# Fused attention and two MLPs on one core: a scheduling priority for 30 attention steps

## The chip, the cores and the metric

The kernel runs on one core of a Trainium2 chip. The metric is the device time of one execution in microseconds (us). Five engines work side by side, each through its own queue in order: PE (TensorE, matmuls), ACT (ScalarE), DVE (VectorE), POOL (GpSimd) and SP (SyncE, which here only issues DMAs).

## The reference: what is computed

Attention over 4 batches, 8 heads, 576 tokens and head size 64, then two MLPs over the 2304 tokens of width 512:

```python
cum    = np.cumsum(np.log(np.clip(f, 0.0001, 1.0)), axis=-1)
scores = np.where(causal, -1e9, q @ k.T / np.sqrt(D) + cum[..., :, None] - cum[..., None, :])
x = softmax(scores) @ v                        # heads side by side: 2304 x 512
h = x @ w_in                                   # 512 -> 2048
x = (h * np.tanh(np.log1p(np.exp(h)))) @ w_out # 2048 -> 512
h = x @ w2_in                                  # 512 -> 1024
s = h * softmax(h)
out = ((s - s.mean()) / np.sqrt(s.var() + 1e-6) * g_ln) @ w2_out   # 1024 -> 512
```

## The kernel before

Every operand of a matmul is split into two fp16 halves, a high one and a low one, and each product is three matmuls (high by high, high by low, low by high). Work that makes such halves is what ACT, DVE and POOL do most.

**Attention.** A batch is cut into five row tiles of up to 128 tokens. A step handles 4, 2, 1, 1 and 1 heads in row tiles 0 to 4, so a batch has 30 steps, listed in `seq` (L640). A step passes through these parts:

- `step_s` computes scores on PE into one of three PSUM banks `sp0` to `sp2` (L436, L437, L439).
- `step_r` takes the row maximum on DVE (`nm`, L478, and L491/L492 in row tile 4) and the exponentials on ACT (`p`, L480, and L494/L495 in row tile 4).
- `step_h` makes the high half of the probabilities on ACT (`ph`, L518) and the low half on POOL (L519), and issues a transposing DMA from SP (`pT`, L524), for two heads at once in row tiles 2 to 4.
- `step_pv` multiplies by the values on PE (`pv`, L550 to L552), three steps after the scores. After the last head `fin` divides (L565), splits the tile (L568 on DVE, L569 on POOL) and issues the transpose `xT` from SP (L577), which the first MLP reads.

`ahead`, called behind the scores, prepares what comes later: the raw loads of the next tile or batch from SP (`rawq`, `rawk`, `rawv`, L317), the sums of squares of the next batch's keys and values on ACT (`jkk`, `jkv`, L331, called the stats below), and the splits of q, k and v.

**First MLP.** It goes through the tokens in blocks of 256, of 8 pairs of 128 hidden columns each. `up` (tiles `h`, L787) is 24 matmuls for one 128-column half, `mish` turns `h` into `gt` (ACT L799, L800, L805 to L807, L813; DVE L804, L808; POOL L814), and `down` (L831, into `x`) multiplies by the second weight. For block 0 the sums of a weight group are taken up by DVE (L842), and at the end `evac` scales and splits the block's result (DVE L853 to L857 and L860, ACT L859) and stores it from SP (`x2d`, L861). The second MLP runs behind it and fills the time after attention is done.

**Weights of the first MLP.** While batch 0's row tiles 2 and 3 and block 0 of the MLP run, the weights are loaded and converted on DVE (L134, L136, L138), measured on PE (`gram`, L157), bounded on DVE (L172 to L177) and split: the high half on ACT (L199), the low half by two fp32 matmuls L206 and one L207 on PE into a score bank, from which ACT takes it (L208).

**What sets the order.** The program text emits steps of attention, weight work and MLP in turns: before the main loop `n0 + LAG` = 9 steps, then step by step between the halves of `up` and `down`. A scheduler then sorts each engine's instructions once, when the kernel is built: of those that are ready in its own timeline it takes the one with the lowest place in the program. Buffers that are allocated once, such as the three score banks, keep the program's order of use. At run time each engine goes through its queue in that fixed order and waits wherever an operand isn't there.

## Time and profile before

| what | us |
|---|---|
| median of 3 runs | 870.66 |
| lowest and highest run | 867.29, 870.78 |
| the profiled execution | 868.76 |
| its span, first to last instruction | 867.0 |
| PE busy in the span | 766.6 (88%) |
| DVE, ACT, POOL busy | 594.2, 563.7, 394.2 |

Read the span as a sequence of stages: loading and the first two row tiles of batch 0 until about 80 us; row tiles 2 to 4 of batch 0 with the weights and block 0 of the first MLP until about 186 us, when block 1 begins; attention and first MLP side by side until about 545 us; and both MLPs without attention from there to the end.

### The profile page before, as it was taken

Reading aid. Unit: us, or ns where it says so; the run is one execution under the profiler, and the core shown is the slowest. Engines: PE = TensorE matmul, PEld = TensorE weight load, DVE = VectorE, ACT = ScalarE, POOL = GpSimd, SP = SyncE. Lnnn points to the kernel's source line nnn. Section 1 sums busy time; section 2 is a strip of 40 time slices with the busy share of each in tenths; the row PEclk is TensorE's granted clock in tenths of the full one; section 3 lists DMA queues with packets and bytes.
Section 4 is the critical chain, followed back from the end, with each engine's and each line's share of the span. In section 5 each row is a group of like instructions: output and inputs, shape, how many; then the busy total and the mean of one; then the engine's idle time right before and its main releaser. Section 6 shows DMA issues by size and latency. Waiting matters only on the chain.

```text
span 867.0 us, 16642 instructions
## 1 busy us (share of the span) xinstructions
PE 766.6 (88%) x6255; PEld 481.0 (55%) x6255; DVE 594.2 (69%) x1160; ACT 563.7 (65%) x1234; POOL 394.2 (45%) x321
## 2 busy tenths in 40 slices
PE   0468998779999997998889899987999999999998
PEld 0335565557667665676556667654555554444443
DVE  6797954668867898669887654689656454666451
ACT  5648687868878877787876666776965544333331
POOL 2232333447876565765678653226733132012110
PEclk9979999969999999999999999998999999999999
DMA  9998544487799968998797542751022424344443
GB/s 242 228 268 251 175 122 80 87 163 144 151 197 172 163 131 149 169 181 148 164 165 121 113 80 56 191 210 61 26 37 61 97 50 73 86 109 99 107 87 85
DMA packets 328573, 114.90 MB, mean 133 GB/s; under 512 B 317676, under 2 KB 317676, under 8 KB 328492
## 3 DMA queue, kind: packets, MB, share of 16 engines
q1 hardware_dynamic: 328492, 113.84, 63.7%
q8 instruction: 49, 0.80, 0.4%
q14 instruction: 32, 0.26, 0.1%
HBM read 46.59 MB, written 9.55 MB: 65 GB/s over the span
## 4 chain that ended last, share of the span: by engine, by line
PE 40%; DVE 19%; DMA 16%; ACT 9%; issue 9%; POOL 6%; SPq 1%; DVEq 0%; POOLq 0%; ACTq 0%
PE h L1030 10%; PE o L1070 10%; PE x L831 7%; PE h L787 7%; DMA pT<-ph 5%; POOL ph L519 3%; DMA wo_r<-in_moe_w_out_dram 2%; DVE ta L804 2%; POOL gt L814 2%; ACT p L480 2%; DMA xT<-xh 1%; DMA w2i_r<-in_moe_w_in_dram 1%; DVE th L808 1%; DVE vt L215 1%; DVE ph L516 1%
## 5 line engine op out<-in xcount | busy, mean ns | idle before, releaser
L831 PE MATMUL x<-wout,gt 128*128 128x512 f16 x864 | 218.4, 386 | 17.0 <-DVE x2h L860 8.4
L787 PE MATMUL h<-xT,win 128*128 128x256 f16 x1728 | 221.0, 279 | 1.8 <-DMA xT<-xh 1.8
L519 POOL TENSOR_TENSOR ph<-p,ph 128x512 f16<-128x512 f32 (+4 forms) x120 | 155.4, 1301 | 92.0 <-ACT ph L518 42.3
L787 PEld LDWEIGHTS <-win 128*128 128x128 f16 x1728 | 170.0, 100 | 45.1 <-issue 5.5
L814 POOL TENSOR_TENSOR gt<-th,gt 128x512 f16<-128x512 f32 x72 | 92.5, 1286 | 128.7 <-ACT gt L813 122.0
L831 PEld LDWEIGHTS <-gt 128*128 128x128 f16 x864 | 80.5, 99 | 96.4 <-issue 12.5
L1058 POOL TENSOR_TENSOR z<-sl,z 128x1024 f16<-128x1024 f32 x18 | 38.7, 2150 | 138.2 <-DVE s2c L1037 111.3
L1030 PE MATMUL h<-w,x2T 128*128 128x512 f16 x432 | 98.0, 379 | 0.9 <-POOL w L222 0.9
L1070 PE MATMUL o<-wo,zT 128*128 128x512 f16 x432 | 96.5, 379 | 0.5 <-DMA zT<-z 0.5
L550 PE MATMUL pv<-vt,pT 128*128 128x64 f16 (+3 forms) x480 | 68.6, 200 | 23.3 <-DMA pT<-ph 22.9
L808 DVE SCALAR_TENSOR_TENSOR th<-ta,th 128x512 f32<-128x512 f32 x72 | 64.6, 898 | 30.5 <-ACT ta L807 28.0
L436 PE MATMUL sp<-kt,qa 128*128 128x128 f16 (+3 forms) x480 | 68.7, 219 | 15.6 <-ACT p L480 9.6
L480 ACT ACTIVATE p<-sp,nm 64x64 f32<-64x64 f32 (+7 forms) x128 | 61.2, 484 | 27.3 <-DVE nm L478 12.9
L813 ACT CAST gt<-th 128x512 f16<-128x512 f32 x72 | 44.4, 616 | 44.2 <-DVE th L808 42.7
L437 PE MATMUL sp<-kt,qb 67*128 67x128 f16 (+3 forms) x480 | 70.5, 219 | 2.5 <-DMA kt<-dd 2.5
L1030 PEld LDWEIGHTS <-x2T 128*128 128x128 f16 x432 | 42.3, 98 | 51.4 <-issue 1.2
L1070 PEld LDWEIGHTS <-zT 128*128 128x128 f16 x432 | 42.2, 98 | 51.5 <-DMA zT<-z 0.9
L804 DVE TENSOR_SCALAR ta<-ta 128x512 f32<-128x512 f32 x72 | 53.7, 746 | 23.5 <-ACT ta L799 23.2
L550 PEld LDWEIGHTS <-pT 128*128 128x128 f16 (+3 forms) x480 | 44.3, 100 | 45.8 <-DMA pT<-ph 29.6
L552 PE MATMUL pv<-vt,pT 128*128 128x64 f16 (+3 forms) x480 | 67.8, 195 | 0.0
L551 PE MATMUL pv<-vt,pT 128*128 128x64 f16 (+3 forms) x480 | 67.8, 195 | 0.0
L805 ACT ACTIVATE ta<-ta 128x512 f32<-128x512 f32 x72 | 45.3, 631 | 34.0 <-DVE ta L804 33.8
(231 smaller groups left out, 1462.6 us busy)
## 6 DMA issues: line engine op xcount, KB each, us to landing
wi_r<-in_moe_w_in_dram SPq DMA_DIRECT2D x8, 1024.0 KB
wo_r<-in_moe_w_out_dram SPq DMA_DIRECT2D x8, 1024.0 KB
rawk<-in_k_dram SPq DMA_DIRECT2D x25, 256.0 KB
rawv<-in_v_dram SPq DMA_DIRECT2D x25, 256.0 KB
x2d<-x2h SPq DMA_DIRECT2D x18, 256.0 KB
out_dram<-ro SPq DMA_DIRECT2D x18, 256.0 KB
w2i_r<-in_moe_w_in_dram SPq DMA_DIRECT2D x4, 1024.0 KB
w2o_r<-in_moe_w_out_dram SPq DMA_DIRECT2D x4, 1024.0 KB
```

What stands on the lines that cost most here:

```text
L436: nc.tensor.matmul(o, qa[:, h, r0:r1_], kc[:, h, a0:a1], start=True, stop=False)
L437: nc.tensor.matmul(o, qb_[:67, h, r0:r1_], kc[:67, H + h, a0:a1], start=False, stop=(c != i))
L480: nc.scalar.activation(pv[:m, g * (i + 1) * P + off:g * (i + 1) * P + end], s3[:, g, off:end], AF.Exp, bias=nm[:m, g:g + 1], accum_out=rs[ ...
L519: nc.gpsimd.tensor_tensor(p4[:, :, 1], pv3, p4[:, :, 0], op=ALU.subtract)
L550: nc.tensor.matmul(o, pT[a0:a1, k, :m], vh, start=(c == 0), stop=False)
L787: nc.tensor.matmul(ph, win[:, (fi // 4) * NC1 + c, col:col + P], x[:, lx * NC1 + c, :], start=(m == 0), stop=(m == 3 * NC1 - 1))
L804: nc.vector.tensor_scalar(ta, ta, E20, 1.0, op0=ALU.min, op1=ALU.add)
L808: nc.vector.scalar_tensor_tensor(th, ta, 2.5, th, op0=ALU.subtract, op1=ALU.mult)
L814: nc.gpsimd.tensor_tensor(gt[:, 1], th, gt[:, 0], op=ALU.subtract)
L831: nc.tensor.matmul(o, gt[:, lg, n % 2, t * P:(t + 1) * P], wout[:, fi, lw * 512:(lw + 1) * 512], start=(first and m == 0), stop=(last and ...
L1030: nc.tensor.matmul(h[:, half * 512:(half + 1) * 512], x[:, lx * NC1 + c, :], self.w2[:, half * NC1 + c, lw * 512:(lw + 1) * 512], start=(n ...
L1070: nc.tensor.matmul(o, zT[:, lz * NF2 + c, :], self.wo[:, c, lw * 512:(lw + 1) * 512], start=(n == 0), stop=(n == 3 * NF2 - 1))
```

## The change

`tc.high_priority(offset=800)` tells the scheduler to rank what is emitted inside it 800 places earlier than where it stands in the program. The change puts it around all parts of steps 6 to 35: row tiles 2 to 4 of batch 0 (24 steps) and row tiles 0 and 1 of batch 1 (6 steps). Around the scores it also covers `ahead` and the `pv` and `fin` of the step three back. No instruction is added or removed; each engine has the same instructions in another order. Line numbers behind the edits are 2 higher at first and 9 higher from the main loop on (L331 becomes L333, L480 L482, L518 L520, L799 L808).

```diff
+HP = 800
+HPN = 30
...
+    def ahead_of(n):
+
+        return tc.high_priority(offset=HP) if n0 <= n < n0 + HPN else nullcontext()
+
     def slot_pre():
 
         n = pos["k"] - 1
         if 0 <= n < len(seq):
-            step_r(*seq[n])
+            with ahead_of(n):
+                step_r(*seq[n])
 
     def slot_mid():
         n = pos["k"] - 1
         if 0 <= n < len(seq):
-            step_h(*seq[n])
+            with ahead_of(n):
+                step_h(*seq[n])
...
     def slot_pe():
         n = pos["k"]
-        if n < len(seq):
-            step_s(*seq[n])
-            b, i, hs = seq[n]
-            for h in hs:
-                ahead(b, i, h)
-        pvs(n - LAG)
+        with ahead_of(n):
+            if n < len(seq):
+                step_s(*seq[n])
+                b, i, hs = seq[n]
+                for h in hs:
+                    ahead(b, i, h)
+            pvs(n - LAG)
         pos["k"] += 1
```

DVE where the last step of batch 0's row tile 2 takes its maxima (`nm_2_6`, `nm_2_7`: heads 6 and 7; `wo_r_969`, `wo_r_982`: the last two pieces of the down weight), before:

```order
L134 TENSOR_SCALAR wout<-wo_r_969 128x1024
L842 SCALAR_TENSOR_TENSOR acc_1478<-x_0_1_4_1596,rho,acc_1478 128x512
L808 SCALAR_TENSOR_TENSOR th_1694<-ta_1693,th_1694 128x512
L478 TENSOR_REDUCE nm_2_6_1006<-sp_146 128x1
L136 SCALAR_TENSOR_TENSOR wout<-wo_r_969,wout 128x1024
L478 TENSOR_REDUCE nm_2_7_1072<-sp_148 128x1
L134 TENSOR_SCALAR wout<-wo_r_982 128x1024
L425 COPY qb_126<-qa_4_1358 64x8x64
L138 SCALAR_TENSOR_TENSOR wout<-wo_r_969,wout 128x1024
L136 SCALAR_TENSOR_TENSOR wout<-wo_r_982,wout 128x1024
```

The same place on DVE in the changed kernel:

```order
L136 TENSOR_SCALAR wout<-wo_r_969 128x1024
L138 SCALAR_TENSOR_TENSOR wout<-wo_r_969,wout 128x1024
L140 SCALAR_TENSOR_TENSOR wout<-wo_r_969,wout 128x1024
L813 TENSOR_SCALAR ta_1745<-ta_1745 128x512
L199 TENSOR_SCALAR wi_d_1003<-ident,wi_b 128x128
L136 TENSOR_SCALAR wout<-wo_r_982 128x1024
L138 SCALAR_TENSOR_TENSOR wout<-wo_r_982,wout 128x1024
L140 SCALAR_TENSOR_TENSOR wout<-wo_r_982,wout 128x1024
L817 SCALAR_TENSOR_TENSOR th_1746<-ta_1745,th_1746 128x512
L480 TENSOR_REDUCE nm_2_6_1006<-sp_146 128x1
```

The two maxima move from between the conversions to behind all of them.

ACT around pairs 6 and 7 of the first MLP's block 0 (`ta_1818` and `ta_1949`; `jkk`, `jkv`: the stats of batch 1's tiles 2 to 4), up to the exponentials of row tile 3, before:

```order
L331 ACTIVATE jkk_2_1456,st_1095<-rawk_2_1391 128x512
L331 ACTIVATE jkv_2_1458,st_1095<-rawv_2_1393 128x512
L331 ACTIVATE jkk_3_1516,st_1095<-rawk_3_1452 128x512
L199 ACTIVATE wout<-wout,wo_b 128x2x512
L799 ACTIVATE ta_1818<-h_12_1762,usc_0_79 128x512
L800 ACTIVATE th_1819<-h_12_1762 128x512
L331 ACTIVATE jkv_3_1518,st_1095<-rawv_3_1454 128x512
L805 ACTIVATE ta_1818<-ta_1818 128x512
L331 ACTIVATE jkk_4_1575,st_1095<-rawk_4_1512 128x512
L806 ACTIVATE ta_1818<-ta_1818,c_k_72 128x512
L807 ACTIVATE ta_1818<-ta_1818 128x512
L199 ACTIVATE wout<-wout,wo_b 128x2x512
```

The same place on ACT in the changed kernel:

```order
L808 ACTIVATE ta_1818<-h_12_1762,usc_0_79 128x512
L809 ACTIVATE th_1819<-h_12_1762 128x512
L201 ACTIVATE wout<-wout,wo_b 128x2x512
L333 ACTIVATE jkk_2_1456,st_1095<-rawk_2_1391 128x512
L814 ACTIVATE ta_1818<-ta_1818 128x512
L808 ACTIVATE ta_1949<-h_14_1843,usc_0_79 128x512
L809 ACTIVATE th_1950<-h_14_1843 128x512
L333 ACTIVATE jkv_2_1458,st_1095<-rawv_2_1393 128x512
L201 ACTIVATE wout<-wout,wo_b 128x2x512
L815 ACTIVATE ta_1818<-ta_1818,c_k_72 128x512
L210 ACTIVATE wout<-sp_147 128x512
L210 ACTIVATE wout<-sp_146 128x512
```

Three stats stood in front of pair 6 and now stand behind its first two instructions; pair 7's first two have moved up, too.

SP where batch 0's last tile of block 1 is transposed (`xT_1234`) and batch 1's raw loads follow, before:

```order
L422 DMA_TRANSPOSE qa_0_1873<-qn_0_1870 128x8x64
L400 DMA_TRANSPOSE kt_0_1866<-kn_125 128x8x64
L577 DMA_TRANSPOSE xT_1234<-xh_3_1650 128x8x128
L317 DMA rawq_1_2112<-in_q_dram 128x8x64
L317 DMA rawk_1_2114<-in_k_dram 128x8x64
L317 DMA rawv_1_2116<-in_v_dram 128x8x64
```

The same place on SP in the changed kernel:

```order
L424 DMA_TRANSPOSE qa_0_1873<-qn_0_1870 128x8x64
L402 DMA_TRANSPOSE kt_0_1866<-kn_125 128x8x64
L319 DMA rawq_1_2112<-in_q_dram 128x8x64
L319 DMA rawk_1_2114<-in_k_dram 128x8x64
L579 DMA_TRANSPOSE xT_1234<-xh_3_1650 128x8x128
L319 DMA rawv_1_2116<-in_v_dram 128x8x64
```

Two raw loads have moved ahead of the transpose.

## Rows read from the trace of the kernel before

**Rows 1.** The page: span, and PE's granted clock in 40 slices.

```profile
span 867.0 us, 16642 instructions
...
PEclk9979999969999999999999999998999999999999
```

**Rows 2.** Windows by stage: busy time of each engine with its instructions, granted clock.

```profile
core 0: us, PE busy (x) PEld busy (x) DVE busy (x) ACT busy (x) POOL busy (x), PEclk, DMA share, GB/s
120.00:160.00 40.00, 35.37 (x266) 21.94 (x265) 21.41 (x45) 30.39 (x62) 13.65 (x9) 0.96 0.42 102
160.00:200.00 40.00, 29.27 (x387) 23.18 (x386) 27.63 (x67) 29.14 (x70) 20.34 (x17) 0.79 0.82 151
200.00:500.00 300.00, 275.61 (x2987) 195.75 (x2986) 239.68 (x424) 229.50 (x573) 208.12 (x187) 0.98 0.86 154
600.00:867.00 267.00, 259.02 (x1333) 130.53 (x1332) 143.83 (x345) 120.09 (x222) 76.90 (x45) 0.99 0.35 76
```

**Rows 3.** Timeline of PE, 133 to 172 us: start, duration, idle before and its releaser.

```profile
133.74 0.35 PE L157 MATMUL gram<-wout 128*128 128x128 bf16 x3 [1.24 <-DVE wout L138]
...
138.24 0.20 PE L550 MATMUL pv<-vt,pT 128*128 128x64 f16 x1 [2.03 <-DMA pT<-ph]
...
171.97 0.20 PE L550 MATMUL pv<-vt,pT 128*128 128x64 f16 x1 [2.20 <-DMA pT<-ph]
```

**Rows 4.** Short windows, columns as in Rows 2.

```profile
140.00:142.00 2.00, 2.00 (x11) 1.43 (x10) 0.13 (x1) 0.60 (x2) 1.79 (x2) 0.50 0.06 12
...
180.00:190.00 10.00, 6.97 (x56) 5.50 (x57) 7.28 (x13) 5.58 (x18) 3.90 (x3) 0.50 0.89 159
```

**Rows 5.** The chain that ended last, in order of time: start, us, what.

```profile
134.49 3.71 DMA pT<-ph
...
146.80 0.72 ACT jkv L331 x2
...
182.99 3.23 DMA xT<-xh
186.26 4.21 PE h L787 x19
```

**Rows 6.** Timeline of ACT, 144 to 157 us.

```profile
144.57 1.15 ACT L199 ACTIVATE wout<-wout,wo_b 128x1024 f16<-128x1024 f32 x1 [0.95 <-DVE wo_b L177]
145.66 0.69 ACT L799 ACTIVATE ta<-h,usc 128x512 f32<-128x512 f32 x1
...
153.56 0.63 ACT L813 CAST gt<-th 128x512 f16<-128x512 f32 x1
...
156.87 0.67 ACT L480 ACTIVATE p<-sp,nm 128x512 f32<-128x512 f32 x1
```

**Rows 7.** Timeline of POOL, 128 to 172 us.

```profile
128.35 6.11 POOL L519 TENSOR_TENSOR ph<-p,ph 128x384 f16<-128x384 f32 x2
...
160.00 1.16 POOL L814 TENSOR_TENSOR gt<-th,gt 128x512 f16<-128x512 f32 x1
161.11 2.27 POOL L519 TENSOR_TENSOR ph<-p,ph 128x512 f16<-128x512 f32 x2
...
169.10 2.27 POOL L519 TENSOR_TENSOR ph<-p,ph 128x512 f16<-128x512 f32 x2 [1.45 <-ACT ph L518]
```

**Rows 8.** Timeline of DVE, 127 to 172 us.

```profile
127.30 0.55 DVE L478 TENSOR_REDUCE nm<-sp 128x1 f32<-128x384 f32 x1
128.05 0.90 DVE L134 TENSOR_SCALAR wout<-wo_r 128x1024 int32<-128x1024 int32 x1 [0.20 <-DMA wo_r<-in_moe_w_out_dram]
...
129.80 1.21 DVE L138 SCALAR_TENSOR_TENSOR wout<-wo_r,wout 128x1024 int32<-128x1024 int32 x1
...
171.31 0.73 DVE L860 SCALAR_TENSOR_TENSOR x2h<-acc,x2m,x2h 128x512 f16<-128x512 f32 x1
```

**Rows 9.** Timeline of SP's DMA issues, 172 to 185 us.

```profile
172.07 0.38 SPq L861 DMA_DIRECT2D x2d<-x2h  x1
172.55 1.91 SPq L524 DMA_TRANSPOSE pT<-ph  x1
...
184.33 0.58 SPq L317 DMA_DIRECT2D rawq<-in_q_dram  x1
184.96 0.64 SPq L317 DMA_DIRECT2D rawk<-in_k_dram  x1
```

More of the change, by code (lines that the diff above doesn't have):

```diff
@@ L1 @@
 import math
-from contextlib import ExitStack
+from contextlib import ExitStack, nullcontext
 import concourse.bass as bass
```

## The prediction, made before the changed kernel was run

> **What bounds the kernel now.** I read the page first for the span and the granted clock by slices [rows 1], then the windows by stage [rows 2]. From 600 us to the end PE is busy 259.02 of 267 us: there it is the bound, it works through a fixed amount, and the end comes as much earlier as PE reaches that stretch earlier. What can be gained or lost is PE's idle time before: 40 - 35.37 = 4.6 us in 120 to 160, 40 - 29.27 = 10.7 us in 160 to 200, and 300 - 275.61 = 24.4 us in 200 to 500 [rows 2]. The other thing that costs is the clock. Behind an idle stretch the granted clock falls to 0.50, which is 1.2 instead of 2.4 GHz: PE waits 2.03 us for a transpose until 138.24 [rows 3] and is at 0.50 in 140 to 142; from 180 to 190 it is at 0.50 throughout, busy 6.97 of 10 us [rows 4]. So an idle microsecond in a stage such as 160 to 190 costs more than itself.
>
> Then I compared the order of both kernels on each engine. The same instructions stand on each; until 80 us nothing differs but swaps of up to 1.4 us between ACT's and DVE's preparations, which I cost at nothing, since PE waits for loads there in either order (1.4 us if it doesn't), and from about 490 us on every queue is identical. Between them moves are local: the same work is done within some 9 us of engine work of its old place, and PE's order comes back to the same cut again and again (for instance just ahead of the last scores of row tile 3, at 163 us). So the change can act only through waits that it closes or opens between 80 and 490 us.
>
> **Part 1, 80 to 142 us: the MLP's first block moves up.** The words of the change would have attention's row tile 2 go earlier. It doesn't: its scores wait for a score bank, and the banks keep the program's order between scores and weight halves. In the new order the scores of heads 6 and 7 stand 5.5 us of PE work later than they did, their pv 5.5 us later, and up and down of block 0 (pairs 4 to 6) 3 to 8 us earlier. What stood idle in front of that pv is then filled: 2.03 us at 138.24, 1.24 us at 133.74 [rows 3], and, with no idle time ahead, the clock need not fall: from 138.8 to 142.4 PE did at half speed what takes 1.8 us at full speed (the window 140 to 142 at 0.50 is the sample [rows 4]). Together 5.1 us. Against this stands a later transpose. On DVE the two maxima now stand behind all conversions of the last two weight pieces. The last piece's landing starts at 128.05 with a 0.90 us operation, then come two of 1.21 us [rows 8]: 131.4. A maximum takes 0.55 us [rows 8]; I add 1.3 us for exponential and cast of the second head and 2.27 us for POOL's pair, which is what the pair took at 161.11 [rows 7]. That gives 135.5 to 135.9, against an issue at 134.49; with the transpose's 3.71 us [rows 5] pv starts at 139.6 instead of 138.24, 1.4 us late but with 5.5 us more work behind it. Net gain at the end of h of pair 6: 5.1 - 1.4 = 3.7 us, so 141.8 instead of 145.5.
>
> The pair's price is where I had to choose. At 128.35 it took 6.11 us, beside three conversions with two operands in SBUF (1.21 us each [rows 8]); at 161.11 and 169.10 it took 2.27 [rows 7]. In the new order it runs behind the conversions, so I take 2.27, and keep 6.11 for the range (rival B).
>
> The Trainium skill, page "SBUF — State Buffer", section "Who interferes with whom", states that a DVE instruction with two SBUF inputs and a GpSimd instruction that reads SBUF exclude each other for the whole instruction. The rows agree: three times 1.21 is 3.6, and 6.11 - 2.27 is 3.84. By that rule the pair takes 2.27 and pv starts at 139.6; without it, at 143.4.
>
> **Part 2, 142 to 163 us: ACT takes most of that back.** In the kernel before, ACT ran without a pause from `ta_1818` at 145.66 to the second exponential of row tile 3 at 156.87: 11.21 us [rows 6]. In the new order that stretch also holds one more high half of a weight (L199, 1.15 us [rows 6], 1.1 between starts), the last cast of `gt` (0.5 between starts, 0.63 alone [rows 6]) and two more stats (0.72 each [rows 5]), which earlier used ACT's pauses in front of it: 11.21 + 1.1 + 0.5 + 1.44 = 14.25 us. 141.8 + 14.25 = 156.0, against 156.87: of 3.7 us 0.8 is left. The sixth stat (0.72) then stands between this exponential and the next, so the casts are level with before. One thing is won: POOL no longer has the low half of `gt` at 160.00 (1.16 us [rows 7]) between the pairs of row tile 3, so the pair at 161.11 ends about 1.0 us earlier. I carry -1.0 to 163 us. Bounds: -3.7 (ACT hides the stats after all) and +3.3 (rival B).
>
> **Part 3, 163 to 190 us.** The transpose of row tile 3's last pair was issued at 172.55, behind the store at 172.07, which waited for DVE's L860 at 171.31 [rows 8, 9]; POOL's pair was done at 169.10 + 2.27 = 171.37 [rows 7]. In the new order L859 stands ahead of this pair's casts on ACT, and the chain to L860 ahead of row tile 4's maxima on DVE, so the store is out earlier and the transpose loses its wait of 1.18 us. With the 1.0 from part 2 it is issued 2.1 us earlier, and the pv that waited 2.20 us for the pair before it [rows 3] gains the 1.0. What is late next is SP: two raw loads (0.58 and 0.64 us [rows 9]) now stand ahead of the transpose `xT`, issued at 182.99 [rows 5]: 2.1 - 1.2 = 0.9 us is left for block 1's first matmuls at 186.26 [rows 5]. They run at 0.50 either way. Ahead of them PE now does eight score matmuls that came after, in its idle time (0.9 us at that clock); I count half. Together -0.9 - 0.5 = -1.4 us. The bounds are -3.5 (the loads cost nothing) and +1.0 (no gain upstream, the loads in full).
>
> **Part 4, 190 to 490 us: shuffles.** Scores and pv move up against up and down by 1 to 5 us of PE work, down of batch 1's first pairs moves back 2.9 us. PE's idle time there is 24.4 us in many pieces of 1 to 2 us [rows 2]. A swap can close one or open one; the trace of before doesn't show which. I take -0.1, with -5 and +5, a fifth of that idle time, as bounds.
>
> **The sum.** -1.4 - 0.1 = -1.5 us (part 1 and 2 are inside part 3's start). The profiled execution took 868.76 us, span 867.0 [rows 1] and 1.76 around it: 867.3. It lies 1.9 us under the median of the runs, so in terms of medians 869.2.
>
> **Rivals.** *A: the work moved up is kept.* If ACT hides the stats, -3.7 us reaches 163 us; with the store out of the way and the loads beside an idle SP, block 1 starts 3.5 us earlier; a fifth of the 24.4 us closes behind it: -3.5 - 4.9 = -8.4, 862.3. For it: PE's queue has work for every one of these gaps, and idle time saved in 160 to 190 is saved at the low clock. Against it: in 145.66 to 156.87 ACT had no pause at all [rows 6], and the chain from there to `xT` is serial.
>
> *B, slower: ACT's full stretch decides.* Part 2's 14.25 us behind `ta_1818` breaks even with 156.87 only if h of pair 6 is done by 142.6. If POOL's pair takes 6.11 us again, pv starts at 143.4 and h is done at 145.7: the exponential starts at 159.9, 3.1 us late, and takes all of row tile 3 with it, up to `xT`. Less 1.2 for the store, plus 1.2 for the raw loads, plus 2 for PE at 0.50 that much longer: +5.1, 875.8. For it: the margin is 0.8 us. Against it: the conversions stand ahead of the maxima on the same engine, so the pair can't overlap them.
>
> *C: the change doesn't do what it says.* With the banks in fixed order attention is not put ahead, moves cancel, and the time is that of before, 870.7, by 2 either way.
>
> **How the numbers follow.** Forecast (-4 to +2 around -1.5) 0.38, A 0.28, B and losses of part 4 of its size 0.24, C 0.10. A measurement of this kernel tells about 0.5%, 4.35 us, from no change. A is faster by more than that, and 0.04 of the forecast; B is slower; the rest is within: 0.32, 0.44, 0.24. The range reaches to just past A and B: 861 to 877.
>
> **What would show it.** In the new profile: pv of row tile 2's last pair at 139 to 140 with no idle time and no fall of the clock ahead of it; that POOL pair near 2.3 us; ACT without a pause from about 142 to 157, six L333 in it; the exponential within 1 us of 156.9; the transpose of row tile 3's last pair at about 170.5 right behind POOL; `xT` at about 182, two raw loads in front; block 1's first matmul at 185.4 at clock 0.50. The prediction is wrong if block 1 starts over 3 us from 186.26, or if PE's idle time in 200 to 500 is over 5 us from 24.4.

## The result, and the profile of the changed kernel

The changed kernel took 874.41 us (median of 13 runs, 871.46 to 877.58), the kernel before 867.04 us beside it (13 runs, 861.62 to 870.78): ratio 1.0087, 95% interval 1.0063 to 1.011, so 0.9% slower. In a second series (e7 below) it was 1.0106, 1.0077 to 1.0135. The time lies in the range (861 to 877), which is luck in part: the range was laid around 870.66 us for the kernel before, and the 13 runs beside this one gave 867.04. The forecast (869.2, 1.5 us faster) missed: the kernel is 7.4 us slower. Rival B, "slower", had +5.1 us, but by another way: it takes POOL's pair at 6.11 us, and the pair took 1.79 (below).

The profiled execution has a span of 875.8 us. First its granted clock in 40 slices, which answers to [rows 1]:

```profile
span 875.8 us, 16630 instructions
...
PEclk9979999959999999999999999998999999999999
```

The windows by stage of the changed kernel, columns as in [rows 2] and [rows 4]:

```profile
140.00:142.00 2.00, 2.00 (x16) 1.41 (x15) 1.41 (x2) 1.80 (x5) 0.54 (x1) 1.00 1.01 195
120.00:145.00 25.00, 24.27 (x188) 14.53 (x187) 15.79 (x30) 17.23 (x31) 5.55 (x6) 1.00 0.42 122
145.00:160.00 15.00, 9.79 (x56) 5.51 (x54) 6.21 (x20) 13.62 (x29) 2.38 (x2) 0.96 0.36 79
200.00:500.00 300.00, 273.75 (x2990) 195.22 (x2988) 240.57 (x423) 231.34 (x578) 204.77 (x187) 0.98 0.87 157
```

Two of these windows in the kernel before:

```profile
120.00:145.00 25.00, 21.52 (x176) 13.98 (x175) 14.79 (x32) 15.60 (x33) 11.38 (x6) 0.93 0.45 117
145.00:160.00 15.00, 13.85 (x92) 7.96 (x91) 6.62 (x14) 14.78 (x30) 2.27 (x3) 1.00 0.37 76
```

PE's idle time didn't go away, it moved. In 120 to 145 us it fell from 25 - 21.52 = 3.5 us to 0.7 us, and the clock in 140 to 142 rose from 0.50 [rows 4] to 1.00: what part 1 promised. In the next 15 us it rose from 1.2 to 5.2 us, and there the granted clock is below 1.00 now. In 200 to 500 us it is 300 - 273.75 = 26.3 us, near the 24.4 of before.

The clock in 140 to 142 is not the order's doing alone. In e4 below, whose order is that of the kernel before up to 180 us, PE waited as long for the same transpose, and the granted clock stayed at 1.00 (in e6, with the same order, it fell again: 0.66 in 140 to 145). A row of PE and the window of e4:

```profile
137.96 0.20 PE L552 MATMUL pv<-vt,pT 128*128 128x64 f16 x1 [2.02 <-DMA pT<-ph]
...
140.00:142.00 2.00, 2.00 (x18) 1.41 (x17) 0.30 (x2) 0.86 (x3) 2.00 (x2) 1.00 0.05 12
```

Where the time went is seen best from fixed points of the program. Here are the microseconds between them in two profiled executions with the order of before (the kernel before, and e6, whose order is the same) and three with the changed order up to 180 us (the changed kernel, its second profiled execution e7, and e12). Two executions of one order tell how much is chance.

| from, to | before | e6 | changed | e7 | e12 |
|---|---|---|---|---|---|
| start of the program, block 0's first `h` | 77.81 | 78.61 | 79.83 | 78.44 | 79.78 |
| that, `ta_1818` of pair 6 on ACT | 67.85 | 69.19 | 66.55 | 65.78 | 65.83 |
| `ta_1818`, second exponential of row tile 3 | 11.21 | 11.19 | 13.49 | 13.48 | 13.50 |
| that, issue of row tile 3's first transpose | 3.20 | 3.19 | 3.86 | 3.85 | 3.86 |
| that, issue of its last transpose | 12.48 | 12.82 | 12.90 | 13.03 | 13.16 |
| that, issue of `xT` | 10.44 | 10.28 | 13.04 | 13.04 | 11.34 |
| `xT`, block 1's first `h` | 3.27 | 3.28 | 3.76 | 3.78 | 4.01 |
| block 1's first `h`, block 3's | 132.31 | 132.43 | 134.03 | 135.49 | 131.42 |
| block 3's, block 6's | 208.79 | 203.74 | 208.87 | 205.20 | 204.39 |
| block 6's, start of the second MLP's last output tile | 330.55 | 330.80 | 330.39 | 331.01 | 331.03 |

Mean of changed and e7 less mean of before and e6: block 1 starts 5.0 us late (192.4 against 187.4 us). Of this 0.9 is there before block 0 begins, where both orders wait for loads and executions of one order differ by 0.8 and 1.4; -2.4 is part 1's gain; +2.3, +0.7, +0.3, +2.7 and +0.5 follow in the five rows below. Blocks 1 and 2 add 2.4 us. The row of blocks 3 to 5 adds 0.8, but two executions of the same order differ there by 5.1 us. The sum is 8.2 us; the timed runs say 7.4 (874.41 - 867.04) and, with e7's ratio, 9.2.

A third execution with the order of before up to 180 us, e4, took 66.59 us in the second row and 12.06 in the third. With it -2.4 becomes -1.7 and +2.3 becomes +2.0: how the time splits at `ta_1818` is in part chance. Their sum is not: from block 0's first `h` to the exponential the order of before took 78.6 to 80.4 us, the changed one 79.3 to 80.0.

Now the engines. ACT of the changed kernel from `ta_1818` to the second exponential of row tile 3 (start, duration; the stats are L333):

```profile
146.38 0.69 ACT L808 ACTIVATE ta<-h,usc 128x512 f32<-128x512 f32 x1 [2.33 <-PE h L796]
...
148.48 0.63 ACT L333 ACTIVATE jkk<-rawk 128x512 f32<-128x512 f32 x1
...
159.36 0.64 ACT L822 CAST gt<-th 128x512 f16<-128x512 f32 x1
159.87 0.72 ACT L482 ACTIVATE p<-sp,nm 128x512 f32<-128x512 f32 x1
...
160.54 0.65 ACT L333 ACTIVATE jkv<-rawv 128x512 f32<-128x512 f32 x1
```

As in [rows 6] there is no pause in it, but it holds five stats instead of three (one is shown), and the sixth stands behind this exponential. PE waits for ACT meanwhile, and later for row tile 3's first transpose: in the timeline of PE (idle time before, and its releaser)

```profile
153.57 1.13 PE L208 MATMUL sp<-wout,wo_d 128*128 128x512 f32 x2 [3.45 <-ACT wout L210]
...
169.64 0.20 PE L552 MATMUL pv<-vt,pT 128*128 128x64 f16 x1 [1.59 <-DMA pT<-ph]
```

The end of the chain, ahead of `xT`, on POOL of the changed kernel: the last pair of row tile 3 (174.17), heads 0 and 1 of row tile 4 (179.47), its head 2 (186.68), then `xh` of row tile 3:

```profile
137.09 1.79 POOL L521 TENSOR_TENSOR ph<-p,ph 128x384 f16<-128x384 f32 x2 [0.38 <-ACT ph L520]
...
174.17 2.43 POOL L521 TENSOR_TENSOR ph<-p,ph 128x512 f16<-128x512 f32 x2 [1.47 <-issue]
179.47 3.20 POOL L521 TENSOR_TENSOR ph<-p,ph 64x640 f16<-64x640 f32 x2 [2.88 <-ACT ph L520]
186.68 1.39 POOL L521 TENSOR_TENSOR ph<-p,ph 64x640 f16<-64x640 f32 x1 [4.01 <-ACT ph L520]
188.04 1.60 POOL L571 TENSOR_TENSOR xh<-x,xh 128x512 f16<-128x512 f32 x1
```

and SP's issues there:

```profile
186.65 1.26 SPq L402 DMA_TRANSPOSE kt<-kn  x1
187.97 0.57 SPq L319 DMA_DIRECT2D rawq<-in_q_dram  x1
188.58 0.58 SPq L319 DMA_DIRECT2D rawk<-in_k_dram  x1
189.66 1.49 SPq L579 DMA_TRANSPOSE xT<-xh  x1
```

The two raw loads stand ahead of `xT` as forecast. But `xT` goes at 189.66, 0.50 us after the second of them is out (188.58 + 0.58), and 0.02 us after POOL finishes `xh` (188.04 + 1.60): what it waited for is POOL, not SP's queue. POOL had waited 4.01 us for ACT's cast of head 2's `ph`, with `xh` queued behind. In the kernel before the same two stand in the same order on POOL, and it cost nothing there:

```profile
173.37 2.77 POOL L519 TENSOR_TENSOR ph<-p,ph 64x640 f16<-64x640 f32 x2 [2.00 <-ACT ph L518]
178.24 1.39 POOL L519 TENSOR_TENSOR ph<-p,ph 64x640 f16<-64x640 f32 x1 [2.10 <-ACT ph L518]
181.60 1.15 POOL L569 TENSOR_TENSOR xh<-x,xh 128x512 f16<-128x512 f32 x1 [1.97 <-DVE xh L568]
```

### The profile page after: what moved, and what is told of

It is laid out like the page before. It is cut to its first block, busy times and chain, and to the rows that moved or that the text cites. A ratio compares the mean times of both kernels' runs of the same rounds, so it can differ in the third digit from the quotient of the medians.

```text
span 875.8 us, 16630 instructions
## 1 busy us (share of the span) xinstructions
PE 771.6 (88%) x6255; PEld 484.0 (55%) x6255; DVE 594.8 (68%) x1160; ACT 563.6 (64%) x1234; POOL 391.6 (45%) x321
## 4 chain that ended last, share of the span: by engine, by line
PE 33%; DVE 10%; DMA 7%; ACT 5%; issue 5%; POOL 3%; SPq 0%; POOLq 0%; ACTq 0%; DVEq 0%
PE h L1039 10%; PE o L1079 10%; PE x L840 6%; PE h L796 5%; DMA pT<-ph 3%; ACT p L482 1%; POOL ph L521 1%; DMA w2i_r<-in_moe_w_in_dram 1%; DVE ta L813 1%; POOL gt L823 1%; DVE th L817 1%; DVE ph L518 1%; DMA kt<-kn 1%; DVE wo L146 1%; DVE wo L140 1%
## 5 line engine op out<-in xcount | busy, mean ns | idle before, releaser
L840 PE MATMUL x<-wout,gt 128*128 128x512 f16 x864 | 222.4, 392 | 18.2 <-DVE x2h L869 8.4
L796 PE MATMUL h<-xT,win 128*128 128x256 f16 x1728 | 218.1, 276 | 2.6 <-DMA xT<-xh 2.1
L521 POOL TENSOR_TENSOR ph<-p,ph 128x512 f16<-128x512 f32 (+4 forms) x120 | 153.5, 1284 | 103.8 <-ACT ph L520 43.7
L552 PE MATMUL pv<-vt,pT 128*128 128x64 f16 (+3 forms) x480 | 70.7, 203 | 21.0 <-DMA pT<-ph 17.8
L817 DVE SCALAR_TENSOR_TENSOR th<-ta,th 128x512 f32<-128x512 f32 x72 | 68.2, 948 | 29.7 <-ACT ta L816 29.4
L482 ACT ACTIVATE p<-sp,nm 64x64 f32<-64x64 f32 (+7 forms) x128 | 61.2, 483 | 32.8 <-DVE nm L480 20.3
L822 ACT CAST gt<-th 128x512 f16<-128x512 f32 x72 | 44.4, 617 | 51.8 <-DVE th L817 50.4
L813 DVE TENSOR_SCALAR ta<-ta 128x512 f32<-128x512 f32 x72 | 53.4, 742 | 24.4 <-ACT ta L808 24.2
L554 PE MATMUL pv<-vt,pT 128*128 128x64 f16 (+3 forms) x480 | 69.9, 198 | 0.0
L553 PE MATMUL pv<-vt,pT 128*128 128x64 f16 (+3 forms) x480 | 69.8, 198 | 0.0
L1050 ACT ACTIVATE e<-h,s2c 128x1024 f32<-128x1024 f32 x18 | 21.7, 1205 | 68.0 <-DVE s2c L1048 68.0
```

What stands on the lines that cost most here:

```text
L482: nc.scalar.activation(pv[:m, g * (i + 1) * P + off:g * (i + 1) * P + end], s3[:, g, off:end], AF.Exp, bias=nm[:m, g:g + 1], accum_out=rs[ ...
L521: nc.gpsimd.tensor_tensor(p4[:, :, 1], pv3, p4[:, :, 0], op=ALU.subtract)
L552: nc.tensor.matmul(o, pT[a0:a1, k, :m], vh, start=(c == 0), stop=False)
L554: nc.tensor.matmul(o, pT[a0:a1, k + 1, :m], vh, start=False, stop=(c == i))
L796: nc.tensor.matmul(ph, win[:, (fi // 4) * NC1 + c, col:col + P], x[:, lx * NC1 + c, :], start=(m == 0), stop=(m == 3 * NC1 - 1))
L817: nc.vector.scalar_tensor_tensor(th, ta, 2.5, th, op0=ALU.subtract, op1=ALU.mult)
```

## The experiments

Three theories were put against each other. *Early:* the loss is made up to block 1, by ACT's full stretch with the stats, and by what hangs on it. *Loads:* the raw loads ahead of `xT`, which the prediction priced, make it. *Late:* the order behind block 1, which part 4 took at nothing, makes it. (In the expectations of e1 to e3 "theory 1" is *early*, and "theory 2" puts the loss ahead of 80 us and behind 190 us.) In the diffs `hi(...)` puts the priority around the named part alone, `later(a, b)` places an instruction behind another in the scheduler's order, without a wait.

**e1, one call of the change alone.** Of all calls under the priority it keeps two raw loads of batch 1 (`rawk`, `rawv` of row tile 2, called in batch 0's row tile 3, head 6). This call alone gives the changed kernel's order on every engine from 80 to 160 us, because on SP it moves the two loads ahead of two weight pieces.

```
+    def hi(k):
+        n = pos['k']
+        return tc.high_priority(offset=HP) if n == 20 and k in 'L' else nullcontext()
...
-                load_raw(b + 1, (6, 8, 14, 15, 16).index(n), "kv")
+                with hi('L'):
+                    load_raw(b + 1, (6, 8, 14, 15, 16).index(n), "kv")
```

> The priority is kept on one call alone: the raw loads of keys and values of batch 1's tile 2, issued in row tile 3's step of head 6. The order is that of the changed kernel on every engine from 80 to 160 us of the kernel before (two raw loads of 0.25 MB ahead of the down weight's pieces 4 and 5 on SP, and all that follows from it), that of the kernel before ahead of 80 us, and another one behind 180 us. Theory 1 (the swap of loads and block 0's new order cost the time): conversion of piece 4 starts about 3.4 us later than in the kernel before, h of pair 6 isn't early, ACT's stretch with five stats puts the second exponential of row tile 3 about 3 us later than 156.9, block 1 starts 3 to 5 us later than 186.3; the total is 4 to 8 us over the kernel before. Theory 2 (the loss arose ahead of 80 us and behind 190 us; block 0's new order is neutral): block 1 starts within 1.5 us of 186.3, the total is within 3 us.

Measured: 875.94 us (6 runs), ratio 1.0124 (1.0098 to 1.0149). One call loses as much as the whole change, and more than the 4 to 8 us expected. Up to block 1 it is the same loss: from `ta_1818` to the exponential 13.48 us, from row tile 3's last transpose to `xT` 13.03 us, block 1 at 191.67 us. Behind 180 us its order is another (137.48 us from block 1 to block 3), so that the totals are alike is partly chance.

**e2, all of the change but that call.**

```
+        return tc.high_priority(offset=HP) if (n0 <= n < n0 + HPN and not (k == 'L' and n == 20)) else nullcontext()
```

> The whole change, but that one call of raw loads keeps its place. The order from 80 to 120 us is that of the kernel before; from 120 us on it differs from both. Theory 1: conversion of piece 4 as in the kernel before, block 1 starts within 2 us of 186.3, the total within 3 us of the kernel before. Theory 2: block 1 is as late as in the changed kernel (about 192) or the total 5 to 9 us over the kernel before.

Measured: 881.9 us (6 runs), ratio 1.0189 (1.0161 to 1.0218), the slowest of all. Up to the exponential it is like the kernel before (10.91 us from `ta_1818`), block 1 starts at 190.66 us, 3.3 us late, and 2.9 of that lie between row tile 3's last transpose and `h` (16.6 us, 13.7 and 13.6 with the order of before). From there to block 6 it takes 348.5 us instead of 341.1 and 336.2. Neither theory had this total. So the early part isn't the only way to lose: the order behind block 1 can cost some 10 us alone.

**e3, the changed kernel with the stats held.** The six stats of batch 1's row tiles 2 to 4 are placed behind row tile 3's third exponential.

```
+    e = nc.scalar.activation(<exponential of p>)
+    if (b, i, h) == (0, 3, 2):
+        sc["exp"] = e
...
+    i = nc.scalar.activation(<stat>)
+    if b == 1 and c >= 2:
+        later(tc, i, sc["exp"])
```

> The changed kernel, with batch 1's stats of tiles 2 to 4 (six operations of ACT, 0.6 us each) issued behind the third exponential of row tile 3. Theory 1 with ACT as the limit: from pair 6's first ACT instruction to row tile 3's second exponential 13.5 - 5 x 0.6 = 10.5 us instead of 13.5; block 1 starts 2 to 3 us earlier than in the changed kernel, the total is 2 to 3 us under it. Rival (the stats only fill, PE's work or POOL decides): the exponential is earlier but block 1 starts within 1 us of the changed kernel. Theory 2: no change at block 1.

Measured: 864.78 us (12 runs), ratio 0.9996 (0.998 to 1.0013). ACT, with L825 to L839 in place of L808 to L822:

```profile
145.62 0.69 ACT L825 ACTIVATE ta<-h,usc 128x512 f32<-128x512 f32 x1 [2.33 <-PE h L813]
...
156.23 0.61 ACT L839 CAST gt<-th 128x512 f16<-128x512 f32 x1
157.05 0.69 ACT L484 ACTIVATE p<-sp,nm 128x512 f32<-128x512 f32 x1 [0.20 <-POOL gt L840]
...
158.39 0.62 ACT L333 ACTIVATE jkk<-rawk 128x512 f32<-128x512 f32 x1
```

From `ta_1818` to the exponential 11.43 us (10.5 expected), 2.1 less: that much the five stats cost there. But block 1 starts at 191.25 us, level with e7 and 1.2 us ahead of the mean of the changed kernel's two executions; about half of what came free is lost again up to there (14.10 us instead of 13.0 from row tile 3's first transpose to its last). The time comes back behind block 1: from its start to block 6's 331.0 us, against 340.7 and 342.9. Whether the held stats do this or the order that they leave there, this run can't tell.

**e4, priority on the raw loads of the next row tile alone** (`rawq`, `rawk`, `rawv`). The order is that of before up to 180 us and from 260 us on.

```
-                load_raw(nb, ni, "qkv")
+                with hi('Q'):
+                    load_raw(nb, ni, "qkv")
```

> The priority is kept on the raw loads of the next tile (q, k, v of batch 1) alone. The order is that of the kernel before up to 180 us, the raw loads stand ahead of the transpose xT of block 1, and from 260 us on the order is again that of the kernel before. If the two loads in front cost their issue time: block 1 starts 1.2 us later than in the kernel before, and of this 0 to 1.5 us is left at 300 us and at the end. If PE's idle time hides them: within 0.5 us at block 1 and at the end.

Measured: 868.01 us (12 runs), ratio 1.0039 (1.0021 to 1.0057). Where nothing else makes `xT` late, the loads ahead of it do cost: 12.04 us from row tile 3's last transpose to `xT` against 10.3 and 10.4, and 3.80 to the first `h` against 3.27 and 3.29. *Loads* has its price here: part 3 took 1.2 us for it, and it is 1.7 up to `xT` and 0.5 behind it. The total, 3 us over the kernel before, is more than the 0 to 1.5 expected; from block 1 to block 3 it took 134.89 us (132.31 and 132.43).

**e5, e1 with the three raw loads of batch 1's first tile held behind row tile 3's third transpose,** to test whether loads beside row tile 3's first transpose make it land late (4.4 us after its issue in the kernel before, 5.9 to 6.1 in the changed order).

```
+    if (b, i) == (0, 3):
+        pend["pt3", h0] = <transpose>
...
+    if (nb, ni) == (1, 0):
+        later(tc, <raw load>, pend["pt3", 4])
```

> The kernel of the one load, with the three half-size raw loads of batch 1's first tile (q, k, v, 64 rows each) issued from SP behind row tile 3's third transpose instead of ahead of its first. PE's order is that of the one-load kernel up to 180 us. Theory 1b (the stats that were moved free the raw buffers later, so that these loads run beside row tile 3's first transposes and slow them): the first transpose of row tile 3 lands 4.4 us behind its issue as in the kernel before instead of 6.1, the cast that waits for it comes 1.5 to 2 us earlier than in the one-load kernel, block 1 starts 1.5 to 2 us earlier than there. Rival (the transposes are slow for another reason, or the loads come back just as late for the splits at 182): landing still 6 us, or block 1 within 0.7 us of the one-load kernel.

Measured: 873.51 us (6 runs), ratio 1.0087 (1.0064 to 1.0111); the transpose landed 6.0 us after its issue, and block 1 came at 193.89 us, 2.2 us later than in e1. The idea fell: with the nearest load 8.6 us ahead of it the landing is as late.

**e6, priority on the maxima, exponentials and casts alone.** Every engine's order is that of the kernel before: a control.

```
+            with ahead_of(n):
+                step_r(*seq[n])
...
+            with ahead_of(n, "h"):
+                step_h(*seq[n])
```

> The priority is kept around the maxima, exponentials and halves (step_r and step_h) alone; each engine's order is then that of the kernel before, instruction for instruction. Time within 0.3% of the kernel before. Its profile is a second look at the old order: where it differs from the first look, the difference is chance; the first look's stretch from 413 to 527 us should be about 3 us shorter here if what the kernel of the raw loads showed there (same order, 3 us less) was chance.

Measured: 866.6 us (10 runs), ratio 1.0012 (0.9995 to 1.003). It gives the table its second column, and the size of chance.

**e7, the changed kernel again,** without any edit.

> The changed kernel once more, for a second look. If the 2.0 us that its first look had lost by 80 us were chance, they are gone here, and all later points move by as much; if they come from the order of the loads at 25 to 35 us, 1 to 2 us are still there.

Measured: 874.43 us (4 runs), ratio 1.0106 (1.0077 to 1.0135). The 13.49, 3.86 and 13.04 us are there again to 0.01 us, and so is the late conversion of the weights (11.15 us after block 0's first `h`, 11.65 in the first execution); of the 7.2 us by which block 1 was late in the first execution, 2.0 was that execution's.

**e8, the kernel before with the stats held,** by the lines of e3 and no priority.

> The kernel before, without any priority, with the six stats issued behind the third exponential of row tile 3, as in the kernel of the held stats. If ACT limits 145 to 157 us in the old order, too, the second exponential comes 1.5 to 2.2 us (three stats) earlier than 156.9. Against it, the raw loads that follow the stats then stand beside row tile 3's transposes. If the first outweighs, block 1 starts 1 to 2 us earlier than in the kernel before and the total is 1 to 3 us under it; if the second, block 1 starts 1 to 3 us later. Behind 190 us the order differs, too, which can add or take several us.

Measured: 875.58 us (5 runs), ratio 1.0108 (1.0086 to 1.013). Holding the stats is no gain of its own: without the priority it makes block 1 start at 194.98 us. The exponential was expected 1.5 to 2.2 us sooner, and it isn't: from `ta_1818` to it 12.27 us, against 11.2 before and in e6 and 12.06 in e4, though no stat is left in that stretch. ACT waits in it for PE and for DVE:

```profile
149.00 1.15 ACT L201 ACTIVATE wout<-wout,wo_b 128x1024 f16<-128x1024 f32 x1 [0.98 <-PE sp L208]
...
156.29 0.62 ACT L839 CAST gt<-th 128x512 f16<-128x512 f32 x1 [0.83 <-DVE th L834]
```

So in that order nothing is won on ACT by holding them; in the changed order 2.1 us are (e3). What e3 won isn't the held stats as such.

**e9, e3 without priority on the raw loads of the next tile** (e4's line left as in the kernel before). From 280 us on its order is that of before.

> The changed kernel with the six statistics of batch 1's row tiles 2 to 4 held behind row tile 3's third exponential, and without priority on the raw loads of the next row tile; from 280 us on its order is that of the kernel before on every engine. Theory of the late order: the early part alone costs what block 1 is late, and behind 280 us nothing is gained or lost. Block 1 at 189.9 us (191.25 of the held kernel less 1.4 for the raw loads that no longer stand ahead of xT), 2.4 us later than the mean of the order of before (186.26 and 188.56), total +2.4 us, ratio 1.003, and at most 1.005. Rival, that holding the statistics is itself worth the time and the other order behind 280 us nothing: ratio 0.998, as the held kernel's 0.9996 less 1.4 us. The landing of row tile 3's first transpose stays at 6.5 us under both.

Measured: 872.37 us (6 runs), ratio 1.0071 (1.0046 to 1.0095). Block 1 starts at 189.51 us, as forecast (189.9), but the total is above the 1.005 allowed. From block 1 to block 3, where its order is still its own, it takes 135.59 us (before 132.31 and 132.43); from block 3 to 6, with the order of before, 203.90 (before 208.79 and 203.74). So e3's 331.0 us behind block 1 belonged to its order there, not to the held stats, and the order between 190 and 280 us is worth 3 us by itself. *Late* was right on where to look, and my figure for it was too small.

**e10, the changed kernel without priority on the raw loads of the next tile.** Its order is the changed kernel's up to 180 us; the edit is the reverse of e4's, in the changed kernel.

> The changed kernel without priority on the raw loads of the next row tile: the order of the changed kernel on every engine up to 180 us, but no raw load ahead of xT; behind 200 us a third order, like neither kernel's. If the accounts are right, xT's issue follows row tile 4's last transpose 1.3 us sooner than in the changed kernel and block 1 starts at 190.1 us on a run whose weights arrive as in the second look at the changed kernel (191.39 less 1.3). Theory of the late order: the total is then block 1's lateness of 2.7 us and whatever the third order brings, anything from -7 to +7 us. Rival, that the order behind block 1 costs nothing and the changed kernel's loss is the early part's alone: total of the changed kernel less 1.3 us, ratio 1.007 to 1.009.

Measured: 869.35 us (12 runs), ratio 1.0041 (1.0021 to 1.006). `xT` did not go sooner: 13.04 us behind row tile 3's last transpose, to the hundredth what the changed kernel has, with one of the two raw loads ahead of it instead of both (none was expected there). SP and POOL of e10:

```profile
186.93 0.40 SPq L319 DMA_DIRECT2D rawq<-in_q_dram  x1
188.14 1.24 SPq L579 DMA_TRANSPOSE xT<-xh  x1
```

```profile
185.16 1.39 POOL L521 TENSOR_TENSOR ph<-p,ph 64x640 f16<-64x640 f32 x1 [4.02 <-ACT ph L520]
186.52 1.59 POOL L571 TENSOR_TENSOR xh<-x,xh 128x512 f16<-128x512 f32 x1
```

SP is free at 187.33 and waits until POOL is done at 188.11. My account of the loads (1.3 us, in the expectation) was wrong for the changed kernel. What the loads do cost is 0.5 us beside `xT`: from `xT` to `h` it is 3.21 here. Behind block 1 the third order took 129.16 us up to block 3 (changed 134.03 and 135.49).

**e11, e1 with the stats held,** the edits of e1 and e3 together.

> Priority on the two raw loads of batch 1's row tile 2 alone, and the six statistics held: the early order of the held kernel on all engines up to 150 us, another order behind block 1. If the statistics' places cause the wait of row tile 3's exponential, the time from the row sums of pair 6 to the second exponential of row tile 3 is 11.4 us as in the held kernel (13.5 with the statistics free). Theory of the late order: block 1 at 190 to 191 us, and a total anywhere from -5 to +10 us beside the held kernel, by the order that the held statistics and the missing priorities leave there. Rival, that the held statistics bring the 8 us of the held kernel whatever stands behind: ratio 0.998 to 1.002.

Measured: 870.72 us (12 runs), ratio 1.0045 (1.0027 to 1.0062). From `ta_1818` to the exponential 10.56 us (11.4 expected), block 1 at 190.11 us; the late order is another again (128.98 us up to block 3). With e3 and e9 this is the third time that holding the stats takes 2 to 3 us out of ACT's stretch in the changed order, and the rival on the total (at most 1.002) fell.

**e12, the changed kernel with one pair turned round on POOL:** `xh` of row tile 3 ahead of head 2's `ph` of row tile 4. Its order is the changed kernel's up to 180 us, and that of before from 220 us on.

```
-    nc.gpsimd.tensor_tensor(p4[:, :, 1], pv3, p4[:, :, 0], op=ALU.subtract)
+    i_ph = nc.gpsimd.tensor_tensor(p4[:, :, 1], pv3, p4[:, :, 0], op=ALU.subtract)
+    if (b, i, hs[0]) == (0, 4, 2):
+        later(tc, i_ph, <low half of xh of row tile 3>)
```

> The changed kernel with one pair put the other way round on POOL: the low half of xh of batch 0's row tile 3 ahead of the low half of ph of head 2 of row tile 4. Its order is the changed kernel's up to 180 us on every engine, and that of the kernel before from 220 us on. In the look with the raw loads no longer ahead of xT (e10) xT was as late as in the changed kernel; there and in the changed kernel POOL ran that ph (1.39 us, behind a 4 us wait for ACT's cast) ahead of xh. Theory: this is what made xT late. Then on a run whose weights arrive as in the second look at the changed kernel, xh is out at 185.6 us, xT goes at 185.9 us right behind kt (187.6 there), 11.3 us behind row tile 3's last transpose (13.04 in the changed kernel, 10.4 before), block 1 starts at 189.2 us (191.39), 1.8 us behind the mean of the order of before, and with the order of before behind 220 us nothing more is lost: ratio 1.002, at most 1.005. Rival, that the wait is DVE's or PE's: xT stays 13 us behind that transpose. Rival on the rest, that the run of order behind block 1 is not what cost the changed kernel its other half: ratio 1.006 or more.

Measured: 871.33 us (12 runs), ratio 1.0051 (1.0032 to 1.0071). POOL and SP:

```profile
186.08 1.15 POOL L573 TENSOR_TENSOR xh<-x,xh 128x512 f16<-128x512 f32 x1 [3.91 <-ACT ph L520]
187.19 1.39 POOL L521 TENSOR_TENSOR ph<-p,ph 64x640 f16<-64x640 f32 x1
```

```profile
186.15 1.26 SPq L402 DMA_TRANSPOSE kt<-kn  x1
187.46 1.30 SPq L583 DMA_TRANSPOSE xT<-xh  x1
```

`xh` is out at 187.23 and `xT` goes right behind `kt`, 11.34 us behind row tile 3's last transpose (11.3 forecast, 13.04 without the turn): this pair made `xT` 1.7 us late. Block 1 starts at 191.47 us, 4.1 us behind the mean of the order of before (forecast 1.8: block 0 began 1.3 us later than in e7, and `h` came 4.01 instead of 3.3 us after `xT`). Behind it blocks 1 to 5 take no longer than with the order of before (131.42 and 204.39 us), and the total is 4.3 us above the kernel before: 1.0051, just over the 1.005 allowed, under the rival's 1.006. So with the late order put back, what is left of the loss is block 1's late start.

## Why the prediction was wrong, step by step

**What was right.** Part 1's mechanism is there: the pv of row tile 2's last pair runs without idle time in front, the clock in 140 to 142 us is 1.00 instead of 0.50 (which e4 had without the change, too), and POOL's pair behind the conversions took 1.79 us (2.27 taken from pairs of 128x512, this one is 128x384; 6.11 before [rows 7]); this is the place of the page "SBUF — State Buffer" of the Trainium skill, section "Who interferes with whom", and the trace agrees with it. Part 2's terms were about right in size: two stats, a cast and a high half more in ACT's stretch made it 13.49 us (14.25 taken), and e3 shows that the five stats in it cost 2.1 us. The store was out of the way of row tile 3's last transpose, as said.

**Rival B was near by luck.** It has the exponential 3.1 us late because POOL's pair takes 6.11 us. The pair took 1.79, the exponential is level with before (from block 0's first `h`), and the loss comes behind it and behind block 1's start. That 874.41 lies near B's 875.8 says nothing for its mechanism.

**Part 1, the gain: 3.7 us taken, 2.4 measured (1.7 with e4).** "Until 80 us nothing differs but swaps" of ACT's and DVE's preparations isn't so: SP's loads at 25 to 50 us stand in another order, too. And just behind 80 us SP issues two raw loads ahead of the fifth and sixth piece of the down weight; the prediction neither lists nor prices this. SP of the changed kernel, then of the kernel before:

```profile
82.56 0.90 SPq L319 DMA_DIRECT2D rawk<-in_k_dram  x1
83.57 0.58 SPq L319 DMA_DIRECT2D rawv<-in_v_dram  x1
84.24 1.44 SPq L123 DMA_DIRECT2D wo_r<-in_moe_w_out_dram  x2
```

```profile
80.59 1.34 SPq L121 DMA_DIRECT2D wo_r<-in_moe_w_out_dram  x2
81.98 0.46 SPq L317 DMA_DIRECT2D rawk<-in_k_dram  x1
82.53 2.83 SPq L317 DMA_DIRECT2D rawv<-in_v_dram  x1
```

DVE, which waits 3 us for the first of these pieces in either kernel, starts it 11.65 and 11.15 us after block 0's first `h` instead of 8.27 and 9.26 (11.1 to 12.2 in the nine profiled executions with this swap, 8.3 to 9.3 in the five without), and PE then waits for DVE (changed kernel):

```profile
91.48 0.69 DVE L136 TENSOR_SCALAR wout<-wo_r 128x1024 int32<-128x1024 int32 x1 [3.04 <-DMA wo_r<-in_moe_w_out_dram]
```

```profile
96.15 0.63 PE L159 MATMUL gram<-wout 128*128 128x128 bf16 x8 [1.97 <-DVE wout L140]
```

So pv started at 144.10 (141.93 in e7) and not at 139.6. That these pieces make the whole 1.3 us is argued, not shown; that the two loads are what makes the new order is shown by e1.

**Part 2, "I carry -1.0 to 163 us": not there.** With ACT's +2.3 the exponential is level with before (measured from block 0's first `h`: 80.04 and 79.26 us, before 79.06 and 80.38), as was forecast within 1 us. But the sixth stat between the exponentials makes the first transpose 0.66 us later behind it, and the 1.0 us from POOL's freed place shows nowhere, since POOL waits 1.31 us for ACT's cast there.

**Part 3 is the step that failed: block 1 taken 1.4 us early, measured 5.0 late.** "The transpose is issued 2.1 us earlier" became 0.3 us later from the first transpose to the last: the store's 1.2 us came free, but row tile 3's first transpose landed 1.5 us later after its issue (5.9 us, before 4.4), and ACT's next casts waited for it, so that the third transpose was issued 8.99 us behind the first (before 7.60). And "what is late next is SP" named the wrong queue. It followed `xT` by its position on SP, where the change moves something, and not by its operand, where nothing moves: on POOL, head 2 of row tile 4 is ahead of `xh` in both orders. Before, that head had been done by 179.63 us and `xh` waited for DVE; now the scores of row tile 4's head 0 stand behind row tile 3's second pv on PE (ahead of it before), and the cast of head 2 stands behind the q, k and v splits on ACT: it starts at 185.83 us against 177.38, 8.4 us later, while row tile 3's last transpose is 4.1 later. ACT and DVE before, then of the changed kernel:

```profile
177.38 0.72 ACT L518 CAST ph<-p 64x640 f16<-64x640 f32 x1 [1.13 <-DMA pT<-ph]
178.92 0.69 DVE L565 TENSOR_TENSOR x<-pv,rr 128x512 f32<-128x512 f32 x1 [1.15 <-PE pv L552]
```

```profile
183.88 0.68 DVE L567 TENSOR_TENSOR x<-pv,rr 128x512 f32<-128x512 f32 x1
185.83 0.72 ACT L520 CAST ph<-p 64x640 f16<-64x640 f32 x1
```

From row tile 3's last transpose to `xT` this costs 2.7 us, 1.7 of it by the turned pair alone (e12). The remaining 1.0 is at DVE by the rows, but no run tests it: before, the division of `x` waits for PE's pv; now the pv is through at 182.8 us (row not shown), and the division comes at 183.88, without idle time, behind the scales of the next batch. DVE came to the rest of those at 182.61, held up by the operation of 1.34 us that the last section shows. An estimate from these rows: had that taken 0.10 us, the pv would have set the division's start, about 1 us sooner.

**Part 4: -0.1 ± 5 us, measured about +3.** The text said that the trace of before can't tell which gap opens; that is so. Of the +3, 2.4 fall between blocks 1 and 3; the other 0.8 is within chance. The runs show that this was the largest unknown: from block 1 to block 3 the orders that were run took 129.0 to 141.5 us, and that of before 132.3 and 132.4. In the chances it had no place of its own: it shared 0.24 with rival B.

**What stays open.** Why row tile 3's first transpose lands 5.9 to 6.2 us after its issue in the changed order, and 6.5 to 6.6 with the stats held, against 4.4 with the order of before and in e2, e5 having ruled out the raw loads just ahead of it. One rival is untested: the next DMA on SP follows 3.3 us behind that transpose in the four executions with 4.4, the second transpose 2.7 us behind in the six with 5.9 to 6.2, and a raw load 3.1 to 3.2 us behind in the four with 6.5 to 6.6. Open, too, is which instruction makes one late order good (e3) and another bad (e2). No run beats the kernel before by more than can be told: e3's 0.9996 is level.

## What to carry to other kernels

A priority around a long stretch of a program acts where an instruction is ready and cheap to move: here two loads, issued some 80 us ahead of the step that calls them, moved past two weight pieces and drew every engine's order up to 160 us after them (e1); so list first what moved earliest, and price that. When something upstream slips, follow each consumer by its operands, also on the queues whose order is unchanged: an instruction that waits in front of another costs nothing until its own input is late. And before a few us are put down to an order, profile the same order twice: here two such executions differ by 5 us in one stretch of 200.

## What the runs showed of the hardware

A DVE operation on 64 x 1 elements with two operands in SBUF (L494, `nm`) took 0.10 us when POOL was idle, and 1.11 and 1.34 us beside POOL's subtractions. DVE of the changed kernel, beside POOL's rows 174.17 (until 176.60) and 179.47 (until 182.67) above:

```profile
174.23 0.68 DVE L493 TENSOR_REDUCE nm<-sp 64x1 f32<-64x512 f32 x1
...
175.49 1.11 DVE L494 TENSOR_TENSOR nm<-nm,ne 64x1 f32<-64x1 f32 x1
...
177.30 0.10 DVE L494 TENSOR_TENSOR nm<-nm,ne 64x1 f32<-64x1 f32 x1
...
181.34 1.34 DVE L494 TENSOR_TENSOR nm<-nm,ne 64x1 f32<-64x1 f32 x1
```

The long ones end at 176.60 and 182.68 us, when POOL's end. So its size doesn't set the time of such an operation; it lasts until the other engine's instruction is through. That holds throughout: in the fourteen profiled executions 139 of these operations took over 0.3 us, and each ends within 0.03 us of the end of an instruction of POOL; the other 309 took at most 0.28 us. The maximum beside POOL (L493, its one operand a score bank in PSUM) took 0.68 us, as it does at 176.53, when POOL is through (row not shown). The same section of the Trainium skill has it so: a DVE instruction with two inputs in SBUF and a GpSimd instruction that reads SBUF exclude each other, and the one that comes second waits for the whole of the first.

The end of the program, from block 6 on, took 330.4 to 331.3 us in all fourteen profiled executions, whatever came before, so a late start there is paid in full, as the prediction assumed.
